# Sums and products moved from VectorE to GpSimd, and a new order of steps, in a Mamba-2 scan with a SwiGLU feed-forward layer

## The chip, the cores and the metric

The kernel runs on one core of one Trainium2 chip. The metric is the time on the device in microseconds (us), the median of several executions. The core has TensorE (PE in the profile; PEld are its weight loads), VectorE (DVE), ScalarE (ACT), GpSimd (POOL) and SyncE (SP), each with an instruction queue of its own that runs in order, and waits on semaphores between them.

## The reference

Two layers follow each other. The first is a Mamba-2 scan over 4 batches, 8 heads and 768 positions, with head size 32 and state size 16, in chunks of 32:

```python
for c in range(nc):
    cum = np.cumsum(la, axis=-1)                       # la = log(clip(a))
    L = np.exp(cum[..., :, None] - cum[..., None, :]) * causal
    M = np.einsum('bhin,bhjn->bhij', Cc, Bc) * L
    y[:, :, sl] = np.einsum('bhij,bhjd->bhid', M, xc) + \
        np.einsum('bhin,bhnd->bhid', Cc, state) * np.exp(cum)[..., None]
    state = decay_full * state + sum_j(B_j x_j * decay_from_j)
```

Its output, transposed to 3072 tokens of 256 values, goes through a feed-forward layer with 1536 hidden values:

```python
xn = x / np.sqrt(np.mean(x * x, -1, keepdims=True) + 1e-6) * rms_g
g, val = xn @ w_gate, xn @ w_val
out = (g / (1 + np.exp(-g)) * val) @ w_out
```

The weights arrive as 64-bit floating point numbers, and all else is computed in 32-bit floating point.

## The kernel before

**Blocks.** The 3072 tokens are six blocks of 512 (block 0 to 5). For each block the scan gives `yt` (with `g`, `L`, `y`, `S`), the norm makes `xn` of it (`sq`, `ms`, `rs`, `rb`, `xn`), and the feed-forward layer makes `hid` and the output of `xn`. The scan of a block runs beside the feed-forward layer of the block before.

**The first block.** The scan starts with the logarithms of `a`. The weights come in 20 pieces of 64-bit words (`fetch`), and each is decoded by ScalarE (`pow`: three activations) and VectorE (`man`: L209 and L212, then `wt`: L218). Block 0 takes its first hidden pairs with plain products (`early` at L855, `gate` at L845), and its output projection is plain as well (`o`, L961, twelve steps of eight matmuls).

**Products with seven multiplications.** For the other hidden pairs of block 0 (j = 3, 4, 5) and for all of blocks 1 to 5, the two products `xn @ w_gate` and `xn @ w_val` are seen as 2x2 blocks and made with seven block products instead of eight: steps `P.k.j` (L929, four matmuls each) for k = 1 to 7 and the pair j. They need sums of weights (`cw`, four sums of 128x256 for each j, L899, tile `sw` and in place `wgv`) and sums of tokens (`tx`, four sums of 128x256 for each block, L906, tile `tx`). ScalarE copies a result out of PSUM (`take`, L935, tile `p`), VectorE adds (`C`, L941, tile `c`, from `val` in PSUM and `p`), ScalarE applies SiLU (`silu`), and VectorE multiplies (`hid`, L954). In a step such as `hid.21` one factor stays in PSUM (`hid<-u,gate`); in `hid.11`, `hid.12` and `hid.22` both are in SBUF (`hid<-c`).

**The output projection of blocks 1 to 5** uses a similar scheme with 3x3-like parts: `O.k.h` (L1050, four matmuls) needs sums of hidden values (`u` on VectorE, `up` on GpSimd, both L1024) and of weights (`two`, `twop`, L1006); `w` adds the products into the output (L1077, L1081), and `put` stores it.

**Decays.** From the third pair of chunks on, the decays of a chunk come from a row spread over partitions by DMA (`spread`), less the sums of its tokens (`sub`, L484), through an exponential (`ex`) and a mask on GpSimd (L492). `L`, `L1` multiply them with products in PSUM.

**What sets the order.** One string, `order`, lists every step as `block:step.numbers`; the steps are issued in that order, so each engine's queue is the sequence of its own instructions in the list. A number behind a slash picks one of three PSUM slots; a slot's next user waits for the readers of the last one. The lists `first_kinds` (block 0) and `kinds` (others) say what a step calls. In the string, a step of block b can belong to a later block's scan: `1:turn.0` works for block 2.

Of the kernel before, what the change touches and what calls it, by code (L numbers as in the profile page):

```python
# [20 lines left out]
def kernel(  # L21
# [930 lines left out]
    def hide_gv(blk, c, j):  # L952
        u, src = (us.pop(j), Xs[j]) if c == 21 else (cs[c, j][:, half[0]], cs.pop((c, j)))
        nc.vector.tensor_tensor(out=hid[:, 2 * j + c // 10 - 1, c % 10 - 1], in0=u,  # L954
                                in1=src[:, half[1]], op=ALU.mult)
# [258 lines left out]
    def of_chunk(n, fn):  # L1214
# [34 lines left out]
        0:turn.1.0 0:Tt.1.1.0 0:Tt.1.0.0 0:sums.1.1 0:T.1.0 0:exp.1.1 0:A.0 0:S.0 0:A.1 0:S.1
        0:g.0.0/0 0:man.0 0:pow.0 0:L.0.0 0:pow.1 0:wt.0 0:last.1 0:man.5 0:mask.1.0/1 0:middles  # L1250
        0:Tl.1 0:sums.1.0 0:never16 0:fetch.4 0:exp.1.0 0:g.1.0/2 0:fetch.3 0:x.4 0:L.1.0 0:last.0
        0:Tl.0 0:scale.2 0:fetch.6 0:g.1.1/0 0:fetch.7 0:man.1 0:pow.5 0:L.1.1 0:y.0/1 0:wt.5 0:sq.0
        0:fetch.12 0:row.1 0:pow.3 0:rowout.1 0:yt.0 0:ydone.0 0:rowe.1 0:y.1/2 0:r.1 0:fetch.13
        0:row.0 0:man.2 0:fetch.9 0:wt.1 0:early.0.0/0 0:parts.1 0:man.6 0:mask.3/1 0:sums.3 0:pow.2
        0:wt.2 0:rowe.0 0:dT.2 0:sq.1 0:ms.0 0:yt.1 0:ydone.1 0:early.0.1 0:man.3 0:wt.3 0:mask.2/2
        0:sums.2 0:pow.6 0:fetch.8 0:wt.6 0:man.4 0:x.2 0:pow.4 0:man.9 0:wt.4 0:rowout.0 0:rs.0
        0:norm.0 0:exp.3 0:pow.9 0:early.1.0/1 0:tok 0:exp.2 1:exps 0:fetch.10 0:early.1.1 0:xn.0
        0:silu.0 0:wt.9 0:tx.0 0:turn.2 1:dT.1 0:T.2 0:Tt.2.1 0:gate.2/0 0:Tt.2.0 0:Td.2 0:tokout
        0:norm.1 0:x.3 0:hid.0 0:pow.10 0:man.8 0:man.10 0:gg.2/1 0:L1.2.3 0:L1.2.2 0:silu.2 0:hid.2
        0:pow.7 0:fetch.11 0:silu.1 0:gate.3/2 0:silu.3 0:pow.8 0:dT.3 0:wt.10 0:A.2 0:man.7 0:wt.7  # L1260
        0:bc.3 0:L.2.0 0:scale.3 0:pow.13 0:S.2 0:hid.3 0:wt.8 0:gate.5/0 0:man.11 0:fetch.14
        0:silu.5 0:hid.5 0:cw.3 0:fetch.18 0:pow.11 0:gate.4/1 0:silu.4 0:hid.4 0:switch.1 0:man.13
        0:fetch.16 0:table.0 0:y.2/2 0:P.2.3 0:switch.0 0:P.1.3 0:wt.11 0:P.1.4 0:pow.12 0:S.3
        0:yt.2 0:take.1.3 0:P.2.4 0:sq.2 0:P.6.3 0:man.14 0:bc.4 0:take.1.4 0:C.11.3 0:take.6.3
        0:wt.13 0:turn.3 0:T.3 0:cw.4 0:Tt.3.1 0:P.5.3 0:Tt.3.0 0:Td.3 0:P.7.3 0:P.6.4 0:take.7.3
        0:C.11.4 1:spread.0 0:gg.3/2 0:silug.11.3 0:C.22.3 0:scale.4 0:P.4.3 0:take.6.4 1:spread.3
        0:x.5 0:L1.3.3 0:P.5.4 0:silug.21.3 0:L.3.0 0:man.12 0:bc.5 0:scale.5 1:table 0:wt.12
        0:L1.3.2 0:P.3.3 0:C.12.3 0:silug.22.3 0:hidg.22.3 0:pow.14 1:bc.0 0:P.7.4 0:wt.14
        0:silug.11.4 0:y.3/2 0:take.7.4 0:pow.16 0:hidg.21.3 0:P.1.5 1:dT.0 1:spread.1 0:P.4.4
        0:fetch.15 0:fetch.17 1:spread.2 0:ydone.2 0:C.22.4 0:P.3.4 0:table.1 1:S.0 0:spread.10  # L1270
        1:S.1 0:take.1.5 0:sq.3 0:hidg.11.3 0:hidg.11.4 0:P.2.5 0:C.11.5 0:yt.3 0:silug.12.3
        1:turn.1 0:silug.21.4 0:ms.1 0:rs.1 0:hidg.12.3 0:o.0/2 0:cw.5 0:P.6.5 1:T.1 1:Tt.1.1
        0:hid.1 1:turn.0 0:man.16 0:wt.16 0:take.6.5 0:P.5.5 0:pow.15 0:man.15 0:wt.15 0:spread.11
        0:P.7.5 0:take.7.5 0:silug.22.4 0:fetch.19 0:C.22.5 0:silug.22.5 0:o.1 0:P.4.5 0:cw.1
        0:silug.21.5 0:C.12.4 0:cw.0 0:hidg.21.4 0:pow.17 1:T.0 0:pow.18 0:rb.1 0:man.19 1:sub.3
        0:o.2 0:hidg.22.5 0:o.3 0:P.3.5 0:C.12.5 0:pow.19 0:silug.12.4 0:o.4 0:man.17 0:o.5 0:xn.1
        1:P.1.1 0:silug.12.5 0:hidg.21.5 1:P.2.1 0:tx.1 1:Tt.0.1 0:hidg.22.4 1:P.1.0 1:take.1.1
        1:C.11.1 1:Tt.0.0 1:P.2.0 0:silug.11.5 1:silu.11.1 0:hidg.11.5 0:hidg.12.5 0:wt.17
        1:take.1.0 1:C.11.0 1:scale2.0 1:silu.11.0 1:P.5.1 1:P.6.0 0:sub.10 0:hidg.12.4 1:P.6.1
        1:take.6.1 0:o.6 0:man.18 0:wt.18 1:two.0 1:P.7.1 1:take.6.0 1:P.7.0 1:take.7.0 0:wt.19  # L1280
        1:two.1 1:P.5.0 0:o.7 1:take.7.1 1:C.22.0 1:x.0 1:P.4.0 1:C.22.1 1:P.4.1 1:silu.22.1
        1:hid.11.0 1:bc.1 1:Tt.1.0 1:Td.1 1:silu.21.1 0:exps 0:o.8 1:cw.2 1:Td.0 1:hid.21.1
        1:silu.21.0 1:P.3.0 1:C.12.0 1:silu.12.0 1:P.1.3 1:hid.21.0 1:take.1.3 1:hid.11.1 0:ydone.3
        1:twop.7 1:hid.12.0 1:P.3.1 1:C.12.1 1:silu.12.1 0:spread.8 0:sub.8 1:P.2.3 1:C.11.3 1:sub.0
        1:two.9 1:P.6.3 1:take.6.3 0:ex.8 1:P.1.2 1:take.1.2 1:P.5.3 1:P.7.3 1:ex.0 1:hid.22.1
        1:P.2.2 1:two.2 1:two.4 1:twop.5 1:scale2.1 1:hid.12.1 1:C.11.2 1:P.6.2 1:take.7.3 1:P.4.3
        1:C.22.3 1:silu.22.3 1:take.6.2 0:o.9 1:silu.22.0 1:sub.2 1:silu.21.3 1:hid.21.3 1:ex.2
        1:P.3.3 1:hid.22.0 0:spread.9 0:sub.9 1:P.7.2 1:take.7.2 1:hid.22.3 1:C.12.3 1:P.1.4
        1:take.1.4 0:sub.11 1:two.10 0:ex.10 0:o.10 0:o.11 1:two.6 0:ex.11 1:silu.12.3 1:P.4.2
        1:two.3 1:twop.8 1:P.5.2 2:bc.1 0:put.0 0:put.3 1:P.6.4 0:put.2 1:silu.21.2 1:silu.11.2  # L1290
# [153 lines left out]
```

## Time and profile before

| | |
|---|---|
| median of 3 executions | 401.04 us (401.02 to 401.68) |
| profiled execution, its time | 402.13 us |
| profiled execution, its span | 400.3 us |
| granted TensorE clock | 0.999 |
| ScalarE busy | 235.6 us (59%) |
| DMA, mean rate over the span | 67 GB/s |

The span is from the first to the last instruction of the profiled execution. Busy time counts overlapping instructions of an engine once. Matmuls overlap: the end of one lies after the start of the next.

### The profile page before, as it was taken

To read this page: it belongs to the slowest core of one execution; us is meant where nothing else is said; L and a number is where in the kernel's file an instruction comes from. 1 tells how busy PE (TensorE), PEld (TensorE's weight loads), DVE (VectorE), ACT (ScalarE), POOL (GpSimd) and SP (SyncE) were. 2 spreads that over 40 slices of the span, in tenths; PEclk is the share of its full clock that TensorE was granted. 3 is DMA by queue.
4 is the path that set the end of the run, shared out by engine and by line. 5 is a ranking of instruction groups with operands and counts; after the bars stand their busy time and mean duration, and the time that the engine had idled before them with its cause. 6 is when DMAs were issued, how large, how long until landed. Compare 5 with 4: busy or idle time off the path is not lost.

```text
span 400.3 us, 9641 instructions
## 1 busy us (share of the span) xinstructions
PE 392.8 (98%) x3841; PEld 333.3 (83%) x3841; DVE 306.6 (77%) x681; ACT 235.6 (59%) x492; POOL 88.6 (22%) x93
## 2 busy tenths in 40 slices
PE   8989999999999999999999999999999999999996
PEld 5656467888888899988889988899988889988996
DVE  5899999999787978677798676687574676656774
ACT  2899898994698561653675473564574551445320
POOL 2210000000158153400042300045501056100222
PEclk9999999999999999999999999999999999999999
DMA  9997978693001216202037400101100001100001
GB/s 112 197 292 201 206 190 121 185 167 37 2 1 67 38 60 121 58 2 44 13 48 144 107 15 10 20 2 48 41 0 3 1 2 33 54 0 2 0 2 53
DMA packets 92469, 27.01 MB, mean 67 GB/s; under 512 B 77416, under 2 KB 86248, under 8 KB 92424
## 3 DMA queue, kind: packets, MB, share of 16 engines
q1 hardware_dynamic: 88264, 26.13, 30.0%
q10 hardware_dynamic: 4160, 0.26, 0.8%
q8 instruction: 30, 0.49, 0.5%
q14 instruction: 15, 0.12, 0.1%
HBM read 22.64 MB, written 3.74 MB: 66 GB/s over the span
## 4 chain that ended last, share of the span: by engine, by line
PE 81%; DVE 13%; ACT 2%; issue 2%; DVEq 0%
PE gate L929 27%; PE o L1050 23%; PE val L929 20%; PE o L961 3%; PE y L716 2%; DVE m L212 2%; DVE wgv L218 1%; DVE m L209 1%; PE g L579 1%; DVE c L941 1%; ACT e L190 1%; DVE sw L899 1%; PE tp L522 1%; DVE hid L878 1%; DVE hid L954 1%
## 5 line engine op out<-in xcount | busy, mean ns | idle before, releaser
L941 DVE TENSOR_TENSOR c<-val,p 128x512 f32<-128x512 f32 x99 | 67.2, 687 | 34.5 <-PE val L929 26.6
L935 ACT COPY p<-gate 128x512 f32<-128x512 f32 x99 | 56.9, 582 | 57.6 <-PE gate L929 50.1
L929 PE MATMUL gate<-tx,wgv 128*128 128x256 f32 x264 | 66.1, 382 | 0.0
L954 DVE TENSOR_TENSOR hid<-c 128x256 f32<-128x256 f32 x99 | 45.6, 478 | 13.6 <-ACT c L190 13.4
L929 PEld LDWEIGHTS gate<-tx,wgv 128*128 128x128 f32 x264 | 49.1, 190 | 7.6 <-ACT p L935 0.8
L190 ACT ACTIVATE c<-c 128x256 f32<-128x256 f32 x99 | 39.5, 414 | 23.8 <-DVE c L941 23.6
L1081 DVE TENSOR_TENSOR ob<-ob,o 128x128 f32<-128x128 f32 (+1 forms) x90 | 23.9, 298 | 17.4 <-PE o L1050 14.5
L1050 PE MATMUL o<-two,hid 128*128 128x128 f32 x280 | 36.8, 277 | 0.0
L1050 PEld LDWEIGHTS o<-two,hid 128*128 128x128 f32 x280 | 34.4, 192 | 1.4 <-DVE hid L954 0.7
L1024 POOL TENSOR_TENSOR s<-hid 128x512 f32<-128x512 f32 x10 | 13.2, 1319 | 98.5 <-DVE hid L954 94.6
L929 PE MATMUL val<-xn,sw 128*128 128x256 f32 x132 | 33.9, 381 | 0.0
L929 PE MATMUL gate<-xn,wgv 128*128 128x256 f32 x132 | 33.3, 382 | 0.5 <-DVE hid L954 0.3
L929 PE MATMUL val<-tx,sw 128*128 128x256 f32 x132 | 33.6, 381 | 0.0
L929 PE MATMUL val<-xn,wgv 128*128 128x256 f32 x132 | 32.9, 381 | 0.7 <-DVE hid L878 0.7
L929 PE MATMUL gate<-tx,sw 128*128 128x256 f32 x132 | 33.2, 383 | 0.0
L492 POOL TENSOR_SCALAR_AFFINE_SELECT L<-L 64x512 f32<-64x512 f32 x32 | 25.3, 790 | 25.5 <-ACT L L190 24.1
L929 PEld LDWEIGHTS val<-xn,wgv 128*128 128x128 f32 x132 | 24.9, 190 | 4.2 <-DVE hid L878 0.8
L768 POOL TENSOR_TENSOR sq<-sq 128x512 f32<-128x512 f32 (+1 forms) x6 | 7.2, 1193 | 94.8 <-ACT sq L190 48.8
L929 PEld LDWEIGHTS gate<-tx,sw 128*128 128x128 f32 x132 | 24.3, 190 | 4.5 <-ACT p L935 0.9
L929 PEld LDWEIGHTS gate<-xn,wgv 128*128 128x128 f32 x132 | 24.4, 190 | 4.3 <-DVE xn L827 0.6
L190 ACT ACTIVATE e<-e,kinks 128x512 f32<-128x512 int16 (+3 forms) x40 | 27.2, 680 | 1.3
L929 PEld LDWEIGHTS val<-tx,sw 128*128 128x128 f32 x132 | 24.7, 190 | 3.7 <-DVE c L941 0.5
(194 smaller groups left out, 715.8 us busy)
## 6 DMA issues: line engine op xcount, KB each, us to landing
...
```

What stands on the lines that cost most here:

```text
L190: nc.scalar.activation(**operands)
L212: nc.vector.scalar_tensor_tensor(out=f, in0=lo.bitcast(U32), scalar=2.0 ** -32, in1=m, op0=ALU.mult, op1=ALU.add)
L492: nc.gpsimd.affine_select(out=L[r], in_=L[r], pattern=[[0, NH], [1, HC]], compare_op=ALU.is_ge, fill=0.0, base=0, channel_multiplier=-1)
L716: nc.tensor.matmul(out=y[2 * k + u][rows, (2 * n + i) * HC:(2 * n + i + 1) * HC], start=(k, u, rows.start) not in opened, stop=True, skip_ ...
L929: nc.tensor.matmul(out=dst[:, half[w]], lhsT=lhsT, rhs=rhs, start=(k in (1, 2, 5) and w == 0), stop=True, skip_group_check=True)
L935: nc.scalar.copy(out=t, in_=Xs[j])
L941: nc.vector.tensor_tensor(out=t, in0=Zs[j], in1=a, op=ALU.add)
L954: nc.vector.tensor_tensor(out=hid[:, 2 * j + c // 10 - 1, c % 10 - 1], in0=u, in1=src[:, half[1]], op=ALU.mult)
L961: nc.tensor.matmul(out=o, lhsT=hid[:, f, k // 2, (k % 2) * P:(k % 2 + 1) * P], rhs=wo[:, f], start=opens, stop=(f == NF - 1), skip_group_c ...
L1024: engine.tensor_tensor(out=hidden_or_sum(o), in0=hidden_or_sum(in0), in1=hidden_or_sum(in1), op=ALU.add if in1[0] == "+" else ALU.subtract)
L1050: nc.tensor.matmul(out=Os[blk, b][:, place * P:(place + 1) * P], lhsT=hidden_or_sum(u)[:, g], rhs=rhs, start=(blk, b) not in opened, stop= ...
L1081: nc.vector.tensor_tensor(out=o, in0=o, in1=src, op=ALU.add if what[0] == "+" else ALU.subtract)
```

## The change

Sums of weights and of tokens become single steps (`cw.j.k`, `tx.k`; k = 0 to 3 is one of the four sums), each of which can be on VectorE or on GpSimd (`cwp`, `txp`). The product with SiLU and the subtraction of the token sums can be on GpSimd too (`hidp`, `hidgp`, `subp`). The arithmetic is the same. From the 30th step on the order is a new one. Over the whole list 13 of 24 weight sums, 16 of 24 token sums, 36 of 132 products and 8 of 16 subtractions are on GpSimd, and of the 80 hidden sums 24 instead of 33.

```diff
-    def subtract(g):
+    def subtract(g, engine=nc.vector):
...
-        nc.vector.tensor_tensor(
+        engine.tensor_tensor(
             out=L, in0=L, in1=tok[:, c, b * NH:(b + 1) * NH].unsqueeze(2).to_broadcast([P, NH, HC]),
             op=ALU.subtract)
...
-    def combine_w(j):
+    def combine_w(j, k, engine=nc.vector):
...
-        for o, in0, in1, op in ((s[:, 0], a21, a22, ALU.add), (s[:, 1], s[:, 0], a11, ALU.subtract),
-                                (a21, a11, a21, ALU.subtract), (s[:, 2], a12, s[:, 1], ALU.subtract)):
-            nc.vector.tensor_tensor(out=o, in0=in0, in1=in1, op=op)
+        o, in0, in1, op = ((s[:, 0], a21, a22, ALU.add), (s[:, 1], s[:, 0], a11, ALU.subtract),
+                           (a21, a11, a21, ALU.subtract), (s[:, 2], a12, s[:, 1], ALU.subtract))[k]
+        engine.tensor_tensor(out=o, in0=in0, in1=in1, op=op)
...
-    def combine_x(blk):
+    def combine_x(blk, k, engine=nc.vector):
...
-        for k, in0, in1 in ((0, b12, b11), (1, b22, t[:, 0]), (2, b22, b12), (3, b21, t[:, 1])):
-            nc.vector.tensor_tensor(out=t[:, k], in0=in0, in1=in1, op=ALU.subtract)
+        in0, in1 = ((b12, b11), (b22, t[:, 0]), (b22, b12), (b21, t[:, 1]))[k]
+        engine.tensor_tensor(out=t[:, k], in0=in0, in1=in1, op=ALU.subtract)
...
-    def hide_gv(blk, c, j):
+    def hide_gv(blk, c, j, engine=nc.vector):
...
-        nc.vector.tensor_tensor(out=hid[:, 2 * j + c // 10 - 1, c % 10 - 1], in0=u,
+        engine.tensor_tensor(out=hid[:, 2 * j + c // 10 - 1, c % 10 - 1], in0=u,
                                 in1=src[:, half[1]], op=ALU.mult)
```

Parts of the new order that the prediction speaks of (the whole list has 1649 steps, before 1613). The start, up to the first large product:

```
0:g.0.1/1 0:L.0.1 0:cx 0:exp.1.1 0:g.0.0/0 0:never16 0:last.1 0:Tl.1
0:turn.1.0 0:Tt.1.0.0 0:fetch.8 0:L.0.0 0:T.1.0 0:Tt.1.1.0 0:mask.1.0/1 0:pow.0 0:A.0
0:fetch.11 0:cc 0:S.0 0:A.1 0:sums.1.0 0:S.1 0:g.1.0/2 0:exp.1.0 0:L.1.0 0:pow.3 0:g.1.1/0
0:eps 0:row.1 0:last.0 0:Tl.0 0:y.0/1 0:rowout.1 0:rowe.1 0:L.1.1 0:scale.2 0:fetch.7 0:wt.0
0:y.1/2 0:fetch.6 0:sq.0 0:pow.1 0:r.1 0:dT.2 0:turn.2 0:yt.0 0:x.2 0:man.3 0:wt.1 0:sq.1
0:yt.1 0:pow.2 0:bc.3 0:parts.1 0:wt.3 0:T.2 0:man.2 0:wt.2 0:mask.3/1 0:man.4 0:early.0.0/0
```

The first products with seven multiplications, and the way to block 1's first product:

```
0:P.2.3 0:switch.0 0:P.2.4 0:P.1.3 0:fetch.12 0:cw.4.0 1:table 0:gg.3/2 0:take.1.3 0:cwp.4.1
0:P.1.4 0:take.1.4 0:tx.0.1 0:cwp.3.2 0:P.6.3 0:L1.3.2 0:take.6.3 0:L.3.0 0:tok 0:L1.3.3
1:dT.1 0:silu.1 0:cwp.4.2 0:C.11.3 0:P.6.4 0:take.6.4 0:P.7.3 0:C.11.4 0:wt.13 0:P.5.3
...
0:P.3.5 0:C.12.5 0:fetch.18 1:turn.1 0:silug.12.5 1:T.1 1:Tt.1.1 0:xn.1 0:silug.21.5 0:o.3
0:cwp.0.2 0:hidg.21.5 1:P.1.0 1:take.1.0 0:txp.1.0 0:txp.1.2 1:P.2.0 0:tx.1.1 1:P.1.1
```

In block 2, and ahead of block 5:

```
2:P.7.4 2:silu.11.5 2:take.7.4 2:spread.1 2:P.5.4 2:C.22.4 2:silu.22.4 3:bc.1 3:scale2.1
2:P.4.5 2:silu.21.5 2:hid.21.5 2:P.4.4 2:subp.1 2:P.5.5 3:turn.1 2:O.2.0 2:hidp.22.4 2:O.2.1
...
4:w.16 4:O.5.0 4:u.8 4:O.5.1 4:w.18 4:O.1.0 4:u.14 4:O.1.1 4:w.20 4:O.7.0 4:O.7.1 4:xn
5:P.1.0 5:P.1.1 4:up.13 4:w.17 4:txp.0 4:w.14 4:w.15 4:O.14.0 4:O.14.1 4:O.19.0 4:u.15
4:w.22 4:w.19 4:txp.2 4:O.19.1 4:w.23 4:O.10.0 4:O.10.1 5:take.1.0 4:w.24 4:w.25 4:txp.1
4:tx.3 5:P.6.0 5:P.2.0 5:take.1.1 5:P.6.1 5:take.6.0 5:take.6.1 5:P.7.0 4:w.21 5:C.11.0
```

More of the change, by code (lines that the diff above doesn't have):

```diff
@@ L1249 @@
[L1249 to L1290, printed above, removed]
@@ L1399 @@
-        5:u.14 5:O.14.0 5:O.14.1 5:O.19.0 5:w.19 5:O.19.1 5:w.22 5:w.23 5:put.3 5:w.21 5:w.24
-        5:put.1 5:up.15 5:O.10.0 5:O.10.1 5:w.25 5:put.2
+        0:mask.0.0/0 0:whole 0:hmask 0:tmask 0:part 0:gcol 0:part2 1:exps 0:after2 0:mask.0.1/1
+        0:fetch.3 0:aT 0:sel 0:la0 0:turn.0.1 0:T.0.1 0:Tt.0.1.1 0:log4.4.2 0:mask.1.1/2 0:Tt.0.0.1
+        0:fetch.4 0:log4.0.4 0:r.0 0:parts.0 0:log 0:d 0:dx 0:log4.6.2 0:turn.0.0 0:Tt.0.0.0
+        0:Tt.0.1.0 0:sums.0.1 0:exp.0.1 0:fetch.2 0:middles 0:T.0.0 0:sums.1.1 0:scale.0 0:sums.0.0
@@ new lines @@
+        0:yt.1 0:pow.2 0:bc.3 0:parts.1 0:wt.3 0:T.2 0:man.2 0:wt.2 0:mask.3/1 0:man.4 0:early.0.0/0
+        0:mask.2/2 0:man.5 0:ms.0 0:x.3 0:pow.4 0:rs.0 0:xn.0 0:sums.3 0:txp.0.0 0:tx.0.2 0:sums.2
+        0:row.0 0:exp.3 0:Tt.2.0 0:Tt.2.1 0:fetch.9 0:Td.2 0:rowe.0 0:early.0.1 0:norm.0 0:pow.5
+        0:exp.2 0:early.1.0/1 0:wt.5 0:early.1.1 0:silu.0 0:rowout.0 0:wt.4 0:fetch.10 0:man.6
+        0:man.7 0:pow.7 0:norm.1 0:A.2 0:S.2 0:hid.0 0:gate.2/0 0:bc.5 0:table.0 0:pow.6 0:wt.7
+        0:man.9 0:wt.6 0:gg.2/1 0:L1.2.3 0:L.2.0 0:silu.2 0:scale.3 0:man.8 0:pow.8 0:pow.9 0:hid.2
@@ new lines @@
+        0:gate.3/2 0:L1.2.2 0:wt.8 0:silu.3 0:hid.3 0:wt.9 0:pow.10 0:man.10 0:gate.4/1 0:y.2/2
+        0:fetch.15 0:man.11 0:silu.4 0:wt.10 0:table.1 0:ydone.1 0:pow.11 0:ydone.0 0:S.3 0:sq.2
+        0:scale.5 0:hid.4 0:yt.2 0:cw.3.0 0:cwp.3.1 0:gate.5/0 0:silu.5 0:wt.11 0:hid.5 0:cw.3.3
+        0:dT.3 0:turn.3 0:T.3 0:Tt.3.0 0:fetch.13 0:switch.1 0:Tt.3.1 0:Td.3 0:pow.13 0:man.13
+        0:P.2.3 0:switch.0 0:P.2.4 0:P.1.3 0:fetch.12 0:cw.4.0 1:table 0:gg.3/2 0:take.1.3 0:cwp.4.1
+        0:P.1.4 0:take.1.4 0:tx.0.1 0:cwp.3.2 0:P.6.3 0:L1.3.2 0:take.6.3 0:L.3.0 0:tok 0:L1.3.3
@@ new lines @@
+        1:dT.1 0:silu.1 0:cwp.4.2 0:C.11.3 0:P.6.4 0:take.6.4 0:P.7.3 0:C.11.4 0:wt.13 0:P.5.3
+        0:tokout 0:take.7.3 0:fetch.14 0:pow.12 0:x.4 0:P.7.4 0:txp.0.3 0:P.4.3 0:man.14
+        0:silug.11.4 0:C.22.3 0:silug.22.3 0:hidgp.22.3 0:bc.4 0:scale.4 0:man.12 0:x.5 0:P.3.3
+        0:wt.12 0:silug.21.3 0:y.3/2 0:hidg.21.3 0:pow.14 0:P.1.5 0:C.12.3 0:P.2.5 1:S.0 1:S.1
+        0:spread.10 0:spread.8 0:fetch.19 0:take.7.4 0:take.1.5 0:cwp.5.0 0:fetch.16 0:cwp.5.1
+        0:spread.11 0:sq.3 0:P.5.4 0:fetch.17 0:C.22.4 0:P.6.5 0:hidgp.11.4 0:yt.3 0:wt.14
@@ new lines @@
+        0:take.6.5 0:cw.5.2 0:silug.12.3 0:P.4.4 0:ms.1 0:hidgp.12.3 0:C.11.5 0:silug.21.4 0:rs.1
+        1:spread.0 0:hidg.21.4 0:man.15 0:exps 0:hid.1 0:o.0/2 0:P.7.5 0:cw.1.0 0:cwp.4.3 0:P.3.4
+        0:cw.1.1 0:C.12.4 0:pow.15 0:wt.15 0:cw.1.2 1:turn.0 1:T.0 0:silug.11.3 0:hidg.11.3
+        0:silug.11.5 0:silug.12.4 0:hidg.12.4 0:take.7.5 0:rb.1 0:pow.16 0:P.5.5 0:o.1 0:o.2
+        0:C.22.5 0:silug.22.4 0:man.16 0:P.4.5 0:silug.22.5 0:cw.1.3 0:cwp.5.3 0:cw.0.0 0:hidgp.11.5
+        0:P.3.5 0:C.12.5 0:fetch.18 1:turn.1 0:silug.12.5 1:T.1 1:Tt.1.1 0:xn.1 0:silug.21.5 0:o.3
@@ new lines @@
+        0:cwp.0.2 0:hidg.21.5 1:P.1.0 1:take.1.0 0:txp.1.0 0:txp.1.2 1:P.2.0 0:tx.1.1 1:P.1.1
+        0:ydone.3 0:wt.16 0:cwp.0.1 0:hidgp.22.4 1:P.6.0 1:P.2.1 1:bc.1 1:C.11.0 0:man.17 1:Tt.1.0
+        1:take.1.1 1:silu.11.0 1:P.6.1 1:take.6.1 1:cwp.2.0 0:o.4 1:C.11.1 1:P.5.1 0:hidgp.12.5
+        1:hid.11.0 0:hidgp.22.5 0:man.19 1:take.6.0 0:pow.19 0:wt.19 1:silu.11.1 1:P.7.1 1:take.7.1
+        0:subp.10 0:txp.1.3 1:P.5.0 1:P.7.0 0:spread.9 1:P.4.1 1:C.22.1 1:P.3.1 1:Tt.0.0 1:silu.22.1
+        1:spread.3 1:hidp.22.1 1:Td.1 1:take.7.0 1:C.22.0 1:silu.21.1 1:P.4.0 0:pow.17 0:cw.0.3
@@ new lines @@
+        1:P.3.0 1:hid.21.1 0:man.18 1:silu.21.0 1:hid.11.1 1:C.12.0 0:ydone.2 1:spread.2 1:hid.21.0
+        1:sub.0 1:cwp.2.2 1:P.1.2 0:sub.8 1:take.1.2 0:o.5 0:wt.17 1:C.12.1 1:sub.3 1:silu.12.0
+        0:pow.18 1:hid.12.0 0:wt.18 1:two.2 1:cwp.2.1 1:P.6.2 1:Tt.0.1 1:P.1.3 1:take.1.3 1:take.6.2
+        1:P.2.2 1:two.3 0:sub.11 1:P.2.3 1:P.7.2 1:silu.22.0 0:o.6 1:P.6.3 1:hid.22.0 0:o.7 1:x.0
+        1:take.7.2 1:C.11.2 1:C.11.3 1:cw.2.3 1:P.5.2 2:dT.0 1:scale2.1 1:two.11 1:sub.2 1:ex.0
+        0:sub.9 1:two.0 1:silu.11.2 1:P.4.2 1:take.6.3 0:ex.9 0:ex.8 1:two.1 1:twop.4 1:silu.11.3
@@ new lines @@
+        1:take.6.4 1:take.6.5 1:L 1:twop.8 1:L1.2 1:P.7.4 1:P.7.5 1:hid.11.5 1:P.5.4 1:take.7.4
+        1:take.7.5 1:P.4.4 1:P.4.5 1:silu.12.2 1:two.5 1:C.22.4 1:y.0 1:silu.22.4 1:hid.11.4
+        1:hidp.12.2 1:silu.21.5 1:hid.21.5 1:u.1 2:S.0 1:P.5.5 1:hid.22.4 1:silu.21.4 1:hid.21.4
+        1:u.0 1:two.7 1:C.22.5 1:P.3.4 1:O.2.0 1:silu.22.5 1:C.12.4 1:silu.12.4 1:O.2.1 1:hid.22.5
+        1:O.15.0 1:O.15.1 1:w.0 1:w.2 2:bc.1 1:x.1 1:u.2 1:y.1 2:S.1 1:P.3.5 1:C.12.5 1:O.3.0
+        1:subp.1 1:O.3.1 1:sq 2:spread.2 1:yt 1:silu.12.5 1:O.0.0 1:O.0.1 1:hidp.12.5 1:O.6.0 1:up.9
@@ new lines @@
+        3:silu.22.0 3:silu.21.0 3:P.5.1 3:P.3.0 3:hid.21.0 3:hid.11.0 3:spread.1 4:dT.1 3:silu.21.1
+        3:hid.21.1 3:subp.0 2:put.1 3:spread.3 3:sub.3 2:table 3:C.12.0 3:C.22.1 3:silu.22.1 3:g
+        3:subp.1 3:P.1.3 3:take.1.3 3:hidp.22.0 3:P.1.2 3:P.2.3 3:C.11.3 2:put.3 3:take.1.2 3:L1.2
+        3:silu.11.3 3:hid.11.3 3:P.6.3 3:P.3.1 3:C.12.1 3:P.6.2 3:take.6.3 3:P.7.3 3:take.7.3
+        3:hidp.22.1 3:take.6.2 3:P.5.3 3:C.22.3 3:P.2.2 3:silu.12.0 3:P.7.2 3:hidp.12.0 3:take.7.2
+        3:C.11.2 3:silu.22.3 3:hidp.22.3 3:P.4.3 3:L 3:L1.3 3:P.5.2 3:C.22.2 3:silu.21.3 3:hid.21.3
```

238 lines of the change are left out of this document (116 added, 122 removed).

## Prediction

> **What bounds the kernel now.** I read the page's busy shares and slices first, then the same by stage, then TensorE's timeline and waits, and last one meeting of GpSimd with VectorE.
>
> ```profile
> PE 392.8 (98%) x3841; PEld 333.3 (83%) x3841; DVE 306.6 (77%) x681; ACT 235.6 (59%) x492; POOL 88.6 (22%) x93
> PE   8989999999999999999999999999999999999996
> DVE  5899999999787978677798676687574676656774
> POOL 2210000000158153400042300045501056100222
> ```
>
> TensorE is busy everywhere, VectorE is nearly full from slice 3 to slice 10 (some 20 to 100 us), and GpSimd does almost nothing just there. By stage (columns as in the busy line, then clock and DMA):
>
> ```profile
> 26.00:38.00 12.00, 11.39 (x119) 8.12 (x118) 11.72 (x25) 11.73 (x18) 0.73 (x1) 1.00 0.81 245
> 38.00:56.00 18.00, 17.32 (x219) 8.09 (x218) 17.06 (x38) 16.02 (x28) 0.00 (x0) 1.00 0.94 205
> 56.00:90.00 34.00, 33.49 (x329) 27.86 (x327) 33.12 (x78) 30.66 (x64) 1.45 (x2) 1.00 0.78 159
> 100.00:380.00 280.00, 279.96 (x2744) 249.31 (x2744) 202.42 (x426) 153.22 (x331) 75.79 (x69) 1.00 0.15 33
> ```
>
> A busy TensorE could still be a stretched one, so I take the distances between starts (start, duration, instruction, count):
>
> ```profile
> 23.92 0.86 PE L694 MATMUL y<-L,xr 128*32 128x128 f32 x24 [0.80 <-DVE L L618]
> 26.07 1.89 PE L855 MATMUL gate<-yt,wgv 128*128 128x256 f32 x8
> ...
> 60.80 1.03 PE L929 MATMUL val<-tx,sw 128*128 128x256 f32 x4
> 61.66 1.03 PE L929 MATMUL gate<-tx,wgv 128*128 128x256 f32 x4
> 62.52 1.03 PE L929 MATMUL gate<-tx,sw 128*128 128x256 f32 x4
> ...
> 86.13 3.62 PE L961 MATMUL o<-wo,hid 128*128 128x256 f32 x16
> 89.99 1.13 PE L929 MATMUL gate<-xn,wgv 128*128 128x256 f32 x4 [0.25 <-DVE xn L827]
> ```
>
> Four matmuls every 0.86 us, 215 ns each, so they really follow each other. From the first large product, early.0.0 at 26.07, TensorE loses only single waits: 0.7 us for hid L878 at 55, 0.3 at 69, 0.4 for xn at 90 (its work ends at 86.13 + 16 x 0.216 = 89.59, it goes on at 89.99), 0.4 at 393. From 100 to 380 us it has 0.04 us of listed idle time. So a gain must come from the start, where TensorE waits for a chain, and from the stretch to 90 us, where VectorE is as full as TensorE. It can be some 1% at most; a loss has no such limit.
>
> **The change, by its parts.** Prices are of queued instructions, taken start to start: on VectorE a 128x256 sum 0.34 us (its row says 418 ns), a 128x512 sum 0.60 (687), a decode of a weight piece 0.95 to 1.07. GpSimd's 128x256 sum is 0.73 (L757, L768), its 128x512 sum 1.27 alone.
>
> *Engines.* To GpSimd go 13 weight sums, 16 token sums and 36 products with SiLU (65 x 0.73 = 47.5 us) and 8 subtractions (8 x 1.27 = 10.2 us; this operation is not on GpSimd before, the 128x512 sum is the nearest row); 9 of 33 hidden sums come back (-11.4 us). GpSimd goes from 88.6 to about 135 us. VectorE loses 65 x 0.34 + 8 x 0.60 - 9 x 0.60 = 21.5 us. After 100 us this is worth nothing: VectorE has 280 - 202 = 78 us free there, and TensorE none. TensorE's and ScalarE's steps are the same in number, the 26 table loads (1.28 us each) too. Cutting a group of four sums into steps adds no instruction.
>
> *The start.* VectorE's last decay product, L.1.1, releases TensorE at 23.92. In the new order man.5 (1.07 us in the timeline), wt.0 (0.33) and scale.2 (0.33) come after it, one copy (0.20) comes ahead: 1.5 us earlier. man.0 and man.1 now stand ahead of L.0.1; their transfers are issued at 8.29 and 9.18 and such pieces land after a median 5.2 us, at 13.5 and 14.4, against 14.06 at which L.0.1 starts now. That can give back up to 0.5, so I take 1.3. From L.1.1 to early.0.0 it is scale.2, wt.0, yt.0 and then mask.3 (0.33 + 0.33 + 0.78 + 0.60), about 2.1 us as now. mask.3 and turn.2 (0.6 + 0.43) are then done and row.0 (0.44) is not: early.0.0 comes at about 24.8 with 0.6 us more of TensorE's work behind it, a lead of 1.9 us.
>
> *To the first product of six, P.1.3 (56.66 us before).* Up to there the new order has done on TensorE turn.3 and P.2.4 more and tok less: +1.0 us. On VectorE it has done S.3, scale.5, Td.3, wt.11 and three single sums more (1.2 + 0.34 + 0.34 + 0.60 + 1.0) and eight sums of tx.0 and cw.3 less (2.7): +0.8 us. If VectorE had no idle time to give, the lead would be 1.0 - 0.8 = 0.2 us; its idle time from 26 to 56 us is 0.28 + 0.94 = 1.2, so at most 1.4. I take the middle, 0.8.
>
> *To block 1's first product (89.99 before).* TensorE has o.4 and o.5 less ahead of it, 2 x 1.73 = 3.46 us, and arrives at 89.59 - 3.46 - 0.8 = 85.3. The product waits for xn.1 on VectorE. Ahead of xn.1 VectorE has 28 sums and products less and 12 more (16 x 0.34 = 5.4), and wt.16, two decodes and one subtraction later (0.6 + 1.9 + 0.6): 8.5 us in all, so xn.1 is ready at 89.94 - 8.5 = 81.4, plus what 14 new GpSimd operations ahead of it hold VectorE up. That price is open:
>
> ```profile
> 72.96 0.72 POOL L768 TENSOR_TENSOR sq<-sq 128x256 f32<-128x256 f32 x1 [12.19 <-ACT sq L190]
> 73.01 1.29 DVE L954 TENSOR_TENSOR hid<-c 128x256 f32<-128x256 f32 x2
> ...
> L954 DVE TENSOR_TENSOR hid<-c x99: 409/418/1491, 68.4 to 383.6; 128x256 f32<-128x256 f32 x99
> L941 DVE TENSOR_TENSOR c<-val,p x99: 675/685/693, 59.8 to 382.1; 128x512 f32<-128x512 f32 x99
> ```
>
> A product with both inputs in SBUF that meets a GpSimd sum takes up to 1.49 us instead of 0.42; the sum c<-val,p, with one input in PSUM, never takes over 0.69. The four 128x256 GpSimd sums before 100 us held VectorE by 0.08, 0.45, 0.28 and 0.54 us (the longer instruction less its kind's usual 0.69, 0.29, 0.69 and 0.42), mean 0.34. So from both sides 14 x 0.08 = 1.1 to 14 x 0.54 = 7.6 us. I take 0.2 each: the new order sets five PSUM readers in a row (L1.3.2, L.3.0, L1.3.3, C.11.3, C.11.4) beside the sums cwp.4.1, cwp.3.2 and cwp.4.2, and no such row was held before. Then xn.1 is there at 81.4 + 2.8 = 84.2, ahead of TensorE's 85.3, and the wait of 0.4 is gone too.
>
> [...]
>
> *New waits on GpSimd's queue, and the transfers.* In block 2 subp.1 waits for spread.1's transfers (median 3.3 us to landing); behind it stand hidp.22.4 and two hidden sums, and O.2.1 waits for hidp.22.4. From P.5.4 to O.2.1 TensorE has 3 x 0.86 + 0.43 + 0.45 = 3.5 us of work, the chain total, SiLU, product takes 0.69 + 0.41 + 0.73 = 1.8: covered by 1.7 us. SyncE's weight pieces change places within the same six buffers; it has issued each 5 us and more ahead of its decode, and I cost that at nothing. If the cover went, a late 512 KB piece would cost its 5 us once.
>
> **Sum.** Lead 0.8, wait for xn gone 0.4: -1.2 us. The profiled execution took 402.13 us with a span of 400.3, 1.1 us above the median of 401.04; I take the difference off the median: 399.8 us.
>
> **The rivals.** *VectorE is held as long as it is relieved.* 14 operations save 14 x 0.34 on VectorE; if each holds it by h, xn.1 comes at 81.4 + 14h. TensorE's work is level with before at 89.99 - 3.46 = 86.5, so from h = 0.36 the kernel is slower. With 0.50, the mean of the two larger holds seen, xn.1 comes at 88.4: +1.9 us, 402.9. With the whole 0.73 it would be 91.6, +5.1. For it: most decodes and weight sums of this stretch have two SBUF inputs, and VectorE has no idle time there. Against it: the PSUM readers set beside. Chance 0.25. *The lead is used up in 26 to 90 us.* With the lead of 0.2 and h = 0.34 xn.1 (86.2) and TensorE (85.9) meet where before stood; 400.8 to 401.3. Chance 0.20. *A GpSimd result comes late in the blocks.* Ahead of block 5 up.13, txp.0, txp.2 and txp.1 stand in a row before P.6.0: 1.27 + 3 x 0.73 = 3.5 us against 2 x 0.86 + 6 x 0.45 = 4.4 us of TensorE's work. Held GpSimd sums took up to 1.78 instead of 1.27, so two holds use up the cover; at four block ends 0.5 us each give +2, 402.5. VectorE's free time speaks against it. Chance 0.08. The forecast keeps 0.47.
>
> **How the numbers follow.** About 0.2%, 0.8 us, can be told from no change. Faster (below 400.2) is the forecast, 0.47; the second rival is the same, 0.20; the other two are slower, 0.33. Lowest: lead 1.4, 0.4 for xn, 0.8 of later waits: 398.4. Highest: h = 0.54 with xn.1 at 89.0, +2.5, and 0.3 of the blocks: 403.8. Both signs hold much; the forecast's own range is 398.4 to 400.2.
>
> **What would show it.** Right: early.0.0 near 24.8 us; the first L929 product on block 1's tokens near 85.5 with no wait for xn; GpSimd near 135 us and no 0 in its slices 7 to 10; TensorE idle under 0.5 us from 100 to 380. Wrong: that product at 87 or later behind xn, with hid, sw and tx rows on VectorE at 0.6 us and more; or o and gate groups waiting for POOL after 100 us.

## The result, and the profile after

| | before | changed | ratio |
|---|---|---|---|
| first comparison, medians | 401.31 us (401.0 to 402.27) | 399.36 us (397.96 to 399.72) | 0.994 [0.992, 0.996] |
| again, beside the last four kernels | 401.63 us (400.79 to 402.53) | 398.10 us (397.83 to 399.73) | 0.992 [0.990, 0.994] |
| profiled execution, time and span | 402.13, 400.3 us | 399.72, 398.0 us | |

The change makes the kernel faster by 0.6 to 0.8%; 399.8 us had been forecast. First the page of the changed kernel, with the busy line, three rows of slices and the granted clock.

```profile
PE 388.4 (98%) x3841; PEld 333.8 (84%) x3841; DVE 285.0 (72%) x617; ACT 236.2 (59%) x492; POOL 136.0 (34%) x157
PE   8799999999999999999999999999999999999996
DVE  7789999998955877676586565677563577465684
POOL 3110024366094345422276512144712042210121
PEclk9789999999999999999999999999999999999999
```

GpSimd now works in the slices where VectorE was full, and VectorE has lost 21.6 us. In the second and third slices, 10 to 30 us, the granted clock (the PEclk row, in tenths) is down to 7 and 8. By stage (columns as in the busy line, then clock, DMA share and rate):

```profile
5.00:26.00 21.00, 17.84 (x240) 12.62 (x240) 16.94 (x44) 13.07 (x30) 3.33 (x6) 0.84 1.04 208
26.00:38.00 12.00, 11.84 (x142) 8.63 (x140) 11.56 (x26) 11.75 (x20) 1.70 (x2) 1.00 0.89 187
38.00:56.00 18.00, 17.07 (x199) 8.30 (x198) 17.62 (x40) 16.69 (x32) 1.18 (x2) 1.00 0.93 218
56.00:90.00 34.00, 33.93 (x331) 28.77 (x330) 31.61 (x64) 28.71 (x59) 16.65 (x21) 1.00 0.63 150
100.00:380.00 280.00, 279.37 (x2753) 250.59 (x2752) 183.90 (x388) 154.91 (x333) 101.31 (x107) 1.00 0.15 34
```

From 56 to 90 us VectorE is down from 33.12 to 31.61 us and TensorE loses 0.07 us there instead of 0.51. TensorE's timeline gives the places that the prediction named: early.0.0, P.1.3, and block 1's first product.

```profile
26.41 1.89 PE L855 MATMUL gate<-yt,wgv 128*128 128x256 f32 x8
57.02 1.03 PE L931 MATMUL gate<-xn,wgv 128*128 128x256 f32 x4
83.31 1.89 PE L963 MATMUL o<-wo,hid 128*128 128x256 f32 x8
85.04 1.03 PE L931 MATMUL gate<-xn,wgv 128*128 128x256 f32 x4
```

The last line has no wait for xn behind it, where before had one. It comes 4.95 us earlier than before, with 3.46 us of work (o.4, o.5) moved behind it: a lead of 1.5 us. At the last matmul (394.61 against 396.97 us) the lead is 2.4 us. But early.0.0 is 0.3 us later than before, not 1.3 earlier. The timeline of the start shows why:

```profile
12.29 0.29 DVE L209 TENSOR_SCALAR m<-wr 128x256 int32<-128x256 int32 x1 [1.45 <-DMA wr<-in_moe_w_gate_dram]
12.58 1.06 POOL L421 TENSOR_TENSOR early<-early,hmask 128x416 f32<-128x416 f32 x1 [3.87 <-ACT early L190]
12.62 1.30 DVE L212 SCALAR_TENSOR_TENSOR m<-wr,m 128x256 f32<-128x256 uint32 x1
14.50 1.22 DVE L618 TENSOR_TENSOR L<-g,L 128x1024 f32<-128x1024 f32 x1
15.77 1.01 PE L443 MATMUL e<-whole,ident 128*128 128x512 bf16 x2 [2.59 <-DVE L L618]
```

VectorE waits 1.45 us for man.0's weight piece, its second instruction is stretched from 0.43 to 1.30 us beside a GpSimd product (L421, on GpSimd before the change too), and L.0.1 starts at 14.50. mask.1.0 needs the PSUM slot that L.0.1 frees, and TensorE stands for 2.6 us. Then the granted clock is 0.5 for 6.83 us, from 15.26 to 22.08 (0.84 in the mean of 5 to 26 us above). In the first comparison the two executions with a mean clock of 0.996 and more took 397.96 and 398.23 us, the four at 0.990 or 0.991 took 399.30 to 399.72.

### The profile page after: what moved, and what is told of

Same layout as the page of the kernel before. It is cut to its first block, busy times and chain, and to the rows that moved or that the text cites. A ratio compares the mean times of both kernels' runs of the same rounds, so it can differ in the third digit from the quotient of the medians.

```text
span 398.0 us, 9646 instructions
## 1 busy us (share of the span) xinstructions
PE 388.4 (98%) x3841; PEld 333.8 (84%) x3841; DVE 285.0 (72%) x617; ACT 236.2 (59%) x492; POOL 136.0 (34%) x157
## 4 chain that ended last, share of the span: by engine, by line
PE 79%; ACT 9%; DVE 4%; DMA 3%; issue 2%; SPq 1%; DVEq 0%; ACTq 0%
PE gate L931 27%; PE o L1052 22%; PE val L931 20%; PE o L963 4%; ACT e L190 3%; PE y L716 2%; DMA xr<-in_x_dram 2%; PE g L579 1%; DMA wr<-in_moe_w_gate_dram 1%; ACT L184 1%; ACT sq L190 1%; SPq L128 1%; DMA br<-in_B_dram 1%; ACT L L190 1%; PE tp L522 1%
## 5 line engine op out<-in xcount | busy, mean ns | idle before, releaser
L943 DVE TENSOR_TENSOR c<-val,p 128x512 f32<-128x512 f32 x99 | 67.2, 686 | 46.4 <-PE val L931 35.1
L931 PE MATMUL gate<-tx,wgv 128*128 128x256 f32 x264 | 65.3, 380 | 0.0
L956 POOL TENSOR_TENSOR hid<-c 128x256 f32<-128x256 f32 x36 | 28.9, 805 | 106.1 <-ACT c L190 104.1
L956 DVE TENSOR_TENSOR hid<-c 128x256 f32<-128x256 f32 x63 | 28.3, 457 | 17.5 <-ACT c L190 15.6
L931 PEld LDWEIGHTS val<-xn,wgv 128*128 128x128 f32 x132 | 24.8, 190 | 4.0 <-DVE hid L878 0.7
L931 PEld LDWEIGHTS val<-xn,sw 128*128 128x128 f32 x132 | 24.6, 190 | 3.4 <-issue 0.2
```

Of the source, the lines that this page charges most:

```text
L931: nc.tensor.matmul(out=dst[:, half[w]], lhsT=lhsT, rhs=rhs, start=(k in (1, 2, 5) and w == 0), stop=True, skip_group_check=True)
L943: nc.vector.tensor_tensor(out=t, in0=Zs[j], in1=a, op=ALU.add)
L956: engine.tensor_tensor(out=hid[:, 2 * j + c // 10 - 1, c % 10 - 1], in0=u, in1=src[:, half[1]], op=ALU.mult)
```

## The experiments

The theory after the result: the gain comes from GpSimd's relief of VectorE in block 0, the start adds nothing. The rivals: the new order alone carries it; the start does; or it is made in the blocks.

**Order and engines apart.** Two kernels. The first has the new order with every step on the engine of before:

```
-0:txp.0.0 ... 0:cwp.3.1 ... 0:hidgp.22.3 ... 5:hidp.22.5
+0:tx.0.0 ... 0:cw.3.1 ... 0:hidg.22.3 ... 5:hid.22.5        (73 steps; u/up and two/twop as before)
```

> The new order, with every step on the engine it had before (14 of the moved ones stand ahead of xn.1). Theory T (the gain comes from VectorE's relief between 26 and 90 us): VectorE gets 14 x 0.34 = 4.8 us back ahead of xn.1 and loses the 2 to 3 us that GpSimd's operations held it; xn.1 is 1.8 to 2.8 us later, of which its 0.6 us of lead and 0.9 us of idle time hide 1.5: block 1's first product at 85.3 to 86.4 behind xn, total 399.7 to 400.8. Rival A (the order alone carries the gain, and the engines are worth nothing): total 399.4 as with both, first product at 85.0 without a wait.

Measured 429.16 us, ratio 1.0689 [1.0676, 1.0703], over 28 us above both ranges. Block 1's first product comes at 89.73 us, 4.7 behind the changed kernel, although early.0.0 came at 23.57. The second has the order of before with the engines of the change:

```
-0:cw.3 ... 0:tx.0 ... 0:hidg.22.3
+0:cw.3.0 0:cwp.3.1 0:cwp.3.2 0:cw.3.3 ... 0:txp.0.0 0:tx.0.1 0:tx.0.2 0:txp.0.3 ... 0:hidgp.22.3
```

> The order of before, each group of four sums cut into single steps, with every step on the engine that the change gives it. Theory T: the start is as before (early.0.0 at 26.07), VectorE is 2 to 3 us less occupied ahead of xn.1, so the waits of before for hid at 55 (0.7) and for xn at 90 (0.4) shrink or go: 400.2 to 401.0. Rival A (the order carries the gain): 401.3 as before. Rival B (steps that were not ordered for GpSimd come late): over 401.5, with TensorE waiting for POOL.

Measured 421.57 us, ratio 1.0499 [1.0485, 1.0512]. Rival B had the sign, but no theory had the size. Neither half of the change gives anything: alone the order costs 28 us and the engines cost 20; together they save 2 to 3.5. This says what the engines are worth in this one order; what the best order without the moves would reach was not tried, other than by the kernel before itself. TensorE's waits, first with the order alone, then with the engines alone (in total, times, longest):

```profile
PE gate L931 <- DVE sw L900: 6.1, 2, 4.2
PE o L1052 <- DVE hid L956: 2.2, 2, 1.5
PE gate L931 <- DVE hid L956: 2.0, 3, 1.0
```

```profile
PE o L1052 <- DVE s L1026: 3.3, 6, 1.4
PE val L931 <- DVE c L943: 3.2, 4, 1.3
PE o L1052 <- POOL s L1026: 2.1, 1, 2.1
```

In the first TensorE waits for what VectorE now has to do itself, in the second for the sums on VectorE and GpSimd that stand late in queues not arranged for them.

**Which block's moves.** The changed kernel with one part of the moved steps back on VectorE:

```
-1:cwp.2.1 ... 2:subp.1 ... 5:hidp.22.5        (50 steps of blocks 1 to 5)
+1:cw.2.1 ... 2:sub.1 ... 5:hid.22.5
```

> The changed kernel with the 50 moved steps of blocks 1 to 5 back on VectorE; block 0's 23 stay on GpSimd, and so do the 24 hidden sums. The order alone came to 429.2 us, 29.8 over the changed kernel; 4.7 of that were lost up to block 1's first product and 25 behind it. Theory T (the order of each block counts on the engines that it was written for): the same place as the changed kernel up to 85 us, then some 15 to 25 us of short waits for VectorE, 414 to 424. Rival A (the prediction's sentence as it stands: VectorE has 78 us free behind 100 us, so where a step runs is worth nothing there): 399.4 to 400.2, and the 25 us came from the nine hidden sums.

Measured 415.06 us, ratio 1.0335 [1.031, 1.0359]: 15.7 us more than the changed kernel. The first product of block 1 is at 83.34 us, so all of the loss lies behind it. The theory holds. The other 7 us of the order's loss (29.8 less 15.7 and 6.9, below) would lie, if the parts add up, with the hidden sums and the sums of the output weights on the engines of before; they were not tried apart.

```
-0:txp.0.0 ... 0:cwp.3.1 ... 0:hidgp.11.5      (block 0's 23 steps)
+0:tx.0.0 ... 0:cw.3.1 ... 0:hidg.11.5
```

> The changed kernel with only block 0's 23 moved steps back on VectorE. Theory T: block 1's first product 4 to 7 us behind its 85.0 in the changed kernel, because VectorE gets 14 x 0.34 = 4.8 us more ahead of xn.1 and its steps stand in an order that did not count on them; nothing is given back later: 403.5 to 406.5. Rival A (only the 50 moves of the blocks matter): 399.4 to 400.2.

Measured 406.25 us, ratio 1.012 [1.0098, 1.0141]: 6.9 more than the changed kernel, and inside the theory's range. The first product of block 1 stands at 91.44 us, 6.4 later, inside it too. A cleaner pair for block 0 is the order alone against the kernel with block 0's moves: both have early.0.0 at 23.6 to 23.8 and differ up to block 1's first product in nothing else, and that product comes at 89.73 and 83.34. So block 0's moves are worth 6.4 us at that place, in this order. The order needs both parts of the moves; of the 2.4 us that the profile gains, 1.5 are there at block 1's first product.

Why a move is worth more than its duration shows in what TensorE waits for in the kernel with the 50 steps back. First its two largest waits, which the changed kernel does not have, then the place of the longer one:

```profile
PE gate L931 <- DVE sw L900: 3.9, 1, 3.9
PE o L1052 <- POOL hid L1026: 3.1, 2, 1.6
```

```profile
103.20 0.41 DVE L900 TENSOR_TENSOR sw<-sw,wgv 128x256 f32<-128x256 f32 x1
103.76 2.04 PE L931 MATMUL gate<-tx,sw 128*128 128x256 f32 x4 [3.86 <-DVE sw L900]
```

The same weight sum (`cwp.2.1`) in the changed kernel:

```profile
97.16 0.91 POOL L900 TENSOR_TENSOR sw<-sw,wgv 128x256 f32<-128x256 f32 x1
```

On VectorE the sum takes 0.41 us, less than half of what it takes on GpSimd. But it stands there in a queue that has work without a gap from 94.0 to 104.8 us, and so it comes 6 us later. TensorE waits 3.9 us for it, and then its clock is at 0.5 for 6.83 us (the mean of the execution is 0.991), which I estimate from those 6.83 us at 2.9 us more: this one place has nearly half of the loss. At the two waits for hidden sums on GpSimd, those sums in turn waited for a product (L956) that came late on VectorE. VectorE's share of 73% over the whole span says nothing of such places.

VectorE's own waits for a SiLU grow as well, first of the changed kernel, then of the one with the 50 steps back:

```profile
DVE hid L956 <- ACT c L190: 15.6, 16, 2.9
```

```profile
DVE hid L956 <- ACT c L190: 22.0, 23, 4.2
```

A product that stands on VectorE ahead of its SiLU stops VectorE's whole queue until ScalarE is done (16 waits of up to 2.9 us in the changed kernel, 23 of up to 4.2 with the 50 steps back), and GpSimd's products wait 104.1 us for ScalarE in the changed kernel without TensorE being listed as waiting for GpSimd. But the longest of the added waits, 4.2 us at 109 us, follows TensorE's stall and does not cause it. How much of the loss the waits for SiLU make was not tried apart.

**The price of GpSimd beside VectorE.** A second sum behind each moved one ahead of xn.1, into a tile that nobody reads (in combine_w; the same in combine_x and hide_gv):

```
         engine.tensor_tensor(out=o, in0=in0, in1=in1, op=op)
+        if engine is nc.gpsimd and doubled:
+            engine.tensor_tensor(out=spare, in0=wgv[:, :, 0, f1], in1=wgv[:, :, 1, f1], op=ALU.add)
```

> The changed kernel with a second sum of no use, on GpSimd, behind each of the 14 moved steps that stand ahead of xn.1 (into a tile that nobody reads): the price h at which a GpSimd sum holds VectorE. xn.1 has 0.6 us of lead and VectorE some 0.9 us of idle time ahead of it. Theory T (h = 0.2): xn.1 2.8 us later, block 1's first product 1.0 to 1.6 us later, 400.3 to 401.2. Rival A (GpSimd locks VectorE for its whole length, h = 0.73): 10.2 us later, block 1's first product over 8 us later, 407 to 409. Rival B (h = 0.34 as in before): 4.8 us later, 402.4 to 403.2. Rival C (a GpSimd sum costs VectorE nothing): 399.4.

Measured 402.24 us, ratio to before 1.0025 [1.0009, 1.0041]; 2.9 more than the changed kernel's first median, 4.1 more than its second. Block 1's first product is at 87.91. I add up, from 26 us to that product, what VectorE's instructions take beyond the usual duration of their kind: 19 of them are held by 8.15 us in all, against 7 and 2.44 us in the changed kernel. The 14 added sums thus cost 5.7 us, 0.41 each: above theory T's 0.2 and above rival B's 0.34 too. The total is above theory T's range and 0.2 us below rival B's. A hold of VectorE for the whole length of each sum (0.73) is out, and so is none at all. TensorE also waits for late GpSimd steps here, so the total is not VectorE's holds alone:

```profile
PE gate L937 <- POOL tx L912: 0.9, 1, 0.9
PE val L937 <- POOL sw L902: 0.8, 1, 0.8
```

In the changed kernel the 19 GpSimd instructions from 26 us to the same product hold VectorE by those 2.44 us, 0.13 each. The order places them beside VectorE's PSUM readers, as two neighbours on VectorE show: the first has an input in PSUM, the second has both in SBUF. Beside the first GpSimd has a sum at 70.76 us, beside the second one at 71.45, 0.73 us each.

```profile
70.85 0.69 DVE L943 TENSOR_TENSOR c<-val,p 128x512 f32<-128x512 f32 x1
71.46 1.26 DVE L218 SCALAR_TENSOR_TENSOR wo<-m,e 128x512 f32<-128x512 f32 x1
```

The first took its usual time: all 99 of L943's sums took 0.67 to 0.69 us. The second took 1.26 us, against 0.69 in the mean of these six decodes before.

**The start.** First L.0.1 ahead of the two pieces:

```
-0:man.0 0:c*2 0:fetch.5 0:man.1 0:g.0.1/1 0:L.0.1 0:cx
+0:c*2 0:fetch.5 0:g.0.1/1 0:L.0.1 0:man.0 0:man.1 0:cx
```

> The changed kernel with man.0 and man.1 behind L.0.1 instead of ahead of it. Theory T (the start's lead of 1.9 us was lost because L.0.1 stands behind a piece whose transfer lands late, and because TensorE's 2.6 us of idle time there lets the granted clock fall to 0.5 for 6.8 us): L.0.1 starts at about 12.7 instead of 14.50, TensorE waits for it about 0.8 instead of 2.6 us, the clock stays at 1.0, early.0.0 comes at 23.5 to 25 instead of 26.41, and at least 1 us of that is left at the end: 397.4 to 398.4. Rival A (the lead is used up from 26 to 85 us, where VectorE is full): early.0.0 as early, total 399.0 to 399.5.

Measured 398.31 us (397.75 to 399.26), ratio 0.9922 [0.9908, 0.9935]. The clock stayed at 1.0, early.0.0 came at 24.99 and the wait of 2.6 us fell to 0.5. The median is in the theory's range, but in the profiled execution block 1's first product came at 84.58: of 1.4 us gained at early.0.0 only 0.5 was left. That execution is the slowest of the six (399.26 us, inside rival A's range; three took 397.8 to 397.9), so this does not decide between the two. Next, work of no use for TensorE where it waits:

```
-0:turn.1.0
+0:turn.1.0*22
```

> The changed kernel with 22 products of no use on TensorE ahead of turn.1.0's transposes (some 2.4 us), written to the bank that the transposes then overwrite: TensorE has work while it waits for L.0.1, and no wait is taken away. Theory T (TensorE's idle time lowers the granted clock, which costs about 1.4 us): clock 1.0 from 15 to 22 us, early.0.0 at about 25.0 instead of 26.41, total 397.9 to 398.5. Rival A (the clock falls for another reason, or the stretch is set by waits on VectorE and ScalarE and not by TensorE's speed): early.0.0 at 26.2 to 26.6, total 399.2 to 399.8.

Measured 400.11 us (399.59 to 400.65), ratio 0.9968 [0.9957, 0.9979]: the total went against the theory, the places did not. The clock stayed at 1.0, early.0.0 came at 25.00 and block 1's first product at 83.61, 1.4 us ahead of the changed kernel. Most of the lead was lost at one place far behind (rows of the two weight loads left out):

```profile
296.46 0.70 PE L931 MATMUL gate<-tx,sw 128*128 128x256 f32 x2
298.38 0.70 PE L931 MATMUL gate<-tx,sw 128*128 128x256 f32 x2 [1.22 <-issue]
```

In the middle of one product TensorE stands for 1.2 us and the profile shows nothing that it waits for. The changed kernel has no such row there. What holds TensorE, and whether the 44 added instructions have to do with it, was not tried.

Then the slot, with nothing moved:

```
-0:mask.1.0/1 ... 0:g.1.0/2 ... 0:y.0/1 ... 0:y.1/2
+0:mask.1.0/2 ... 0:g.1.0/1 ... 0:y.0/2 ... 0:y.1/1
```

> The changed kernel with four PSUM slots exchanged: mask.1.0 takes slot 2 (free when exp.1.1 ends at 13.4) instead of slot 1 (free when L.0.1 ends at 15.7), g.1.0 takes 1, y.0 takes 2 and y.1 takes 1. No instruction is added, moved or taken away. Theory T (the start's lead was lost behind that one wait, first by the wait and then by the clock that it lowers): TensorE's wait of 2.6 us falls to under 1, the clock stays at 1.0, early.0.0 comes at about 25.0 instead of 26.41 and block 1's first product at 83.6 to 84.3 instead of 85.04: 397.4 to 398.4. Rival A (L.1.0 and L.1.1 on VectorE set the end of the start, not TensorE): early.0.0 within 0.3 of 26.4 and 399.0 to 399.7.

Measured 398.69 us (398.61 to 399.11), ratio 0.9933 [0.9918, 0.9948]. The wait is gone and the clock stays up, but mask.3 then waited 1.9 us for yt.1, so that early.0.0 came at 25.79. Block 1's first product came at 83.97 all the same, inside the theory's range; the total lies 0.3 above it. The same with mask.3 behind early.0.0, and then with the two pieces moved as well:

```
-0:mask.3/1 0:man.4 0:early.0.0/0
+0:man.4 0:early.0.0/0 0:mask.3/1
```

> The four exchanged PSUM slots, and mask.3 one place later, behind early.0.0: with the slots exchanged alone, mask.3 waited 1.9 us for yt.1 and held early.0.0 back to 25.79. Theory T (VectorE, not the start, sets block 1's first product once TensorE is early enough): early.0.0 at 23.4 to 24.2, block 1's first product at 83.2 to 84.0 (83.97 with the slots alone), total 397.6 to 398.7. Rival A (every us of the start comes through): the product at 82.0 to 82.8, total 396.7 to 397.4.

> The same with man.0 and man.1 behind L.0.1, so that VectorE does not wait for man.0's transfer (1.45 us in the changed kernel). Theory T: L.0.1 at 12.7 to 13.7, early.0.0 at 23.2 to 24.4; VectorE has gained at most the 1.45 us: block 1's first product at 82.6 to 84.0, total 397.0 to 398.5. Rival A (the two pieces' decodes then stand ahead of L.0.0 and hold up L.1.0 and L.1.1, as with the pieces alone, where early.0.0 came at 24.99): total 398.3 to 399.2.

Measured 397.98 us (397.78 to 398.72), ratio 0.9914 [0.9898, 0.9929], and 398.96 us (397.68 to 399.12), ratio 0.9929 [0.9913, 0.9944]. In the profiled executions early.0.0 came at 24.07 and 24.42, the product at 84.08 and 84.42, both a little behind theory T's ranges for it. An early.0.0 that is 1.7 us earlier than with the slots alone gave a product no earlier there. But both executions are the slowest of theirs (398.72 and 399.12 us), so for theory T speaks the first kernel's total, inside its range and above rival A's, and not the places. In the last kernel early.0.0 gained nothing over the one before it, and the total is in rival A's range. Neither kernel beats the changed one measured beside it (0.9914 and 0.9929 against 0.992, the intervals overlapping).

**The changed kernel again.**

> The changed kernel once more, unaltered, beside the others on one chip. Theory T (the clock's fall in the start makes two groups of times): executions with a mean clock of 0.996 and more at 397.9 to 398.4, those at 0.990 to 0.992 at 399.2 to 399.8, none between that has the higher clock and the longer time. Rival A (the spread has another cause): the times do not sort by the clock.

Measured 397.84, 397.83 and 397.84 us at a mean clock of 1.0, 398.35 at 0.996, 399.73 and 398.83 at 0.991. They sort by the clock as forecast, though one at 0.991 is below the range that I gave, and the three at 1.0 by 0.07 us too. This profile had 3.41 us at half clock instead of 6.83: block 1's first product came at 83.69 instead of 85.04, and the span is 396.6 instead of 398.0. The same 1.35 us appear at both places: this much of the start does come through.

After the same wait of 2.6 us the clock can also stay up. Windows from 16 to 24 us, of the changed kernel's first profile, of its second, and of the kernel with doubled sums, which has the same start:

```profile
16.00:20.00 4.00, 4.00 (x60) 2.77 (x58) 3.18 (x9) 1.19 (x2) 0.00 (x0) 0.50 0.55 56
20.00:24.00 4.00, 4.00 (x74) 2.90 (x74) 3.32 (x6) 2.28 (x6) 0.00 (x0) 0.74 0.89 338
```

```profile
16.00:20.00 4.00, 4.00 (x63) 2.73 (x62) 3.32 (x10) 1.17 (x2) 0.00 (x0) 0.66 0.58 69
20.00:24.00 4.00, 3.90 (x95) 2.81 (x94) 4.00 (x9) 3.48 (x9) 0.85 (x1) 1.00 0.91 308
```

```profile
16.00:20.00 4.00, 4.00 (x98) 3.13 (x96) 3.86 (x9) 2.48 (x5) 0.00 (x0) 1.00 0.53 64
20.00:24.00 4.00, 3.47 (x75) 2.30 (x64) 3.96 (x10) 3.26 (x8) 0.89 (x2) 1.00 0.88 305
```

The clock is 0.50, 0.66 and 1.00 from 16 to 20 us. Matmuls finished there go from 60 to 98, TensorE "busy" 4.00 each time, and early.0.0 follows at 26.41, 25.08 and 24.38. The busy share says nothing of the clock here.

**The start of before.** The steps up to early.0.0 that both kernels have done by then in the order of before, then the new order:

```
+0:sel 0:mask.1.1/2 0:after2 0:aT 0:kinks 0:la0 0:mask.0.1/1 ... 0:g.0.1/1 0:L.0.1 ... 0:man.1 ... 0:early.0.0/0
 ... (the rest of the new order)
```

> The steps up to early.0.0 in the order of before (those of them that the changed kernel also has done by then), the rest in the new order. Theory T (the gain is made from 26 to 90 us, where GpSimd relieves VectorE, and the start adds nothing at the end): early.0.0 at 25.6 to 26.6, block 1's first product at 84.6 to 86.0, no clock below 0.99, total 399.0 to 400.4. Rival A (the start's new order carries the gain): the product at 86.5 or later, total 400.8 to 402.

Measured 398.99 us (397.6 to 399.61), ratio 0.9926 [0.9908, 0.9945]; early.0.0 at 25.20, block 1's first product at 84.95, no lower clock. early.0.0 is 0.4 earlier than forecast, and 0.9 earlier than before, with man.5, wt.5 and row.0 now behind it. The total lies between the changed kernel's two medians, and its best execution is the shortest of all. So the new order of the start isn't needed for the gain.

This kernel's times lie in two groups too (397.6 and 397.7, the others 399.0 to 399.6), and here the clock is 1.0 in all; what parts them stays open. It lies ahead of block 1's first product, as far as the profiles show: in the seven profiles of the changed kernel and of its other starts, the fillers' left out, TensorE's last eight matmuls begin 308.8 us after that product each time.

## Why the prediction was right, step by step

- **What bounds.** Right. TensorE lost only single waits from early.0.0 on, and the gain to 90 us came where VectorE was full.
- **The start (a lead of 1.9 us, early.0.0 at 24.8).** Wrong in the profiled execution: 26.41. The step that failed is "that can give back up to 0.5, so I take 1.3", on man.0 and man.1 ahead of L.0.1. I set the landing of the pieces against L.0.1's start and stopped there. I missed the held decode (0.9 us), that L.0.1 releases a PSUM slot to mask.1.0, and the clock's fall to 0.5 for 6.83 us behind the 2.6 us of idle time. In the six profiles with this order of the start it came at 23.57 to 26.41, so 24.8 lies among them; and with the start of before the total is the same.
- **To P.1.3 (lead 0.8).** Measured 57.02, 0.36 later than before with 1.0 us more work done: 0.64. The size is right by luck: not 1.9 shrinking to 0.8, but 0.3 growing to 0.6.
- **Block 1's first product (85.3, xn ready at 84.2, no wait).** Measured 85.04; its half of xn was there at 84.5 (83.76 + half of 1.41). Right, and the product did not wait. How near the place came is in part luck: the fall of the clock, which the prediction did not have, moves it, and in the second profile it came at 83.69.
- **GpSimd's price (h = 0.2 each, by the order's PSUM readers).** 0.13 for the instructions as they are placed, 0.41 for the ones added without an order. The reason given for taking less than the mean of before, 0.34, fits: placed beside other steps a GpSimd sum costs three times as much.
- **Engines (GpSimd 135, VectorE 21.5 less).** 136.0 and 21.6. The subtraction that had no row on GpSimd took 1.10 in the mean; 1.27 was taken.
- **"After 100 us this is worth nothing."** The step that failed in its reason. Behind the first product the lead grew by 0.9 us, in no wait: by the starts of the single matmuls, gaps of over 0.2 us are 0.5 us in all before and 1.8 us in the changed kernel, and the gain is in many smaller ones, under 0.2 us each, between products. What makes them smaller was not tried. And VectorE's 78 us of free time would not have covered the steps: with the 50 back on VectorE the new order loses 15.7 us. A step was priced by its duration alone, and not by when its result comes out of the queue that it stands in.
- **New waits on GpSimd's queue, at nothing.** Right; no list has TensorE waiting for GpSimd. Its idle time from 100 to 380 us is 0.63 us, 0.4 for hid on VectorE and 0.2 for ob on ScalarE, where under 0.5 was said.
- **The sum (-1.2).** The medians say 1.95 us at first and 3.5 the second time; four of six executions had the lower mean clock (0.990 or 0.991) at first, two of six the second time. The terms: lead 1.5 instead of 1.2 at block 1, 0.9 more behind it, and a clock that falls in some executions.
